# Holding the square of chunk 2's decays behind the last N eviction of chunk 1 in a chunked RWKV and mixture-of-experts kernel

## The chip, the cores and the metric

The kernel runs on one core of one Trainium2 chip. The metric is device microseconds of one execution, lower is better. The kernel before was run three times, and the numbers of the profile come from one further, profiled execution of the same program.

## The reference

The first half is a linear attention with a matrix state for each batch and head (4 batches, 8 heads, 768 steps, head size 40):

```python
for t in range(S):
    y[:, :, t] = np.einsum('bhd,bhde->bhe', rt, state)
    Sa = np.einsum('bhde,bhe->bhd', state, at)
    state = state * wt[:, :, None, :] - np.einsum('bhd,bhe->bhde', Sa, bt)
    state = state + np.einsum('bhd,bhe->bhde', vt, kt)
```

The second half sends each of the 3072 tokens (320 wide) to the one of 8 experts with the largest gate, computes relu(x @ w1[e]) @ w2[e] with 1024 hidden units, and scales the row by its gate weight and an output gate.

## The kernel before, in words

The 768 steps are cut into 12 chunks of 64 (`C`). Each chunk c goes through these stages:

- `scan(c)` (L103 to L124). The decays `w` and the tile `D` (a, k and b of the reference) are loaded by SyncE's queue (L109, L111). Two scans on VectorE (L116) give the running products `P` and `I`. ScalarE then squares the decays minus 0.9 **in place**, into the tile `w` itself, and keeps their sum (L119); that sum is only read at the very end, by a range check. `w`, `D`, `P` and `I` have one buffer each. So the next chunk's one-column memset of `w` on VectorE (L108) and its load of `w` (L109) have to wait until the square of this chunk is done.
- `prep(c)` (L137 to L249). The products scale a (`Av`, L184, L185, and 24 columns by ScalarE in L187) and k, b (`KBt`, L212). `Av` is spread into `Am`; for chunk 2 ScalarE (L201) and GpSimd (L203) do it, for later chunks transfers (L192). Three transfers a chunk, called the strips here, carry `Av` into the tile `LA` (L178). TensorE multiplies `KBt` by `Am` in six groups (L225); ScalarE copies each group out of PSUM in an "N eviction" of two parts (L236, the mark `s.mark['n', c]` ends as the very last of them) and an `LA` eviction (L238), and GpSimd masks the latter (L240). Transposes into `KB` and `WT` follow (L163, L165).
- `tinv(cs)` (L251). A triangular inverse on VectorE, by many small multiply and reduce pairs (L276, L278, L314 to L322), which starts with a transpose of `N` (L266 for chunks 0 and 1, which go alone; L271 for the later ones, which go in pairs).
- `crit(c, q)` (L367), two for each chunk. The recursion itself: alternating small matmuls (L379, L392), ScalarE moves out of PSUM (L383) and VectorE sums (L405), and the state for the next chunk (L430 to L439). `Dt` (L409) on GpSimd needs the strips of chunk c + 1.
- `tail` and the expert routing write the rows; the experts come last.

Below, square(c), N(c), w(c), D(c) and strips(c) are those of chunk c.

The order on each engine is fixed before the run. The function traces the work, `background()` feeding `prep`, `scan` and `tinv` between the steps of `crit`, and the framework's planner (`tile.TileContext(nc, schedule_with_timeline_sim=True)`, L1157) lays every engine's instructions, SyncE's transfers among them, into one queue each, by the times of its own model. The chip then takes each queue in that order. `tc.issue_after(x)` ties what is traced in its block, as far as it runs on the engine of x, behind x in that engine's queue. `scan(c + 1)` is traced right after `prep(c)` (L506 to L508), so when `scan(2)` is traced, the last N eviction of chunk 1 has been traced and marked. The kernel before already holds square(1) and the copy in L187 of chunk 1 behind the last eviction of N(0).

Of the kernel before, what the change touches and what calls it, by code (L numbers as in the profile page):

```python
# [49 lines left out]
def pat(x, off, dims):  # L50

    return bass.AP(x.tensor, x.offset + off, [x.ap[0]] + [list(d) for d in dims])


class Att:
# [47 lines left out]
    def scan(s, c):  # L103

        nc, V = s.nc, s.nc.vector
        n = 12 * 2 * 33
        w = s.p1.tile([120, n + 1], F32, name="w")
        V.memset(w[:, n:], 0.0)  # L108
        nc.sync.dma_start(out=w[:, 0:n], in_=s.win[c])  # L109
        s.D = s.p1.tile([120, 12, 3, C], F32, name="D")  # L110
        s.mark[c] = nc.sync.dma_start(out=s.D, in_=s.din[c]).ins  # L111
        P, I = (s.p1.tile([120, 12, 2, 33], F32, name=x) for x in "PI")
        Pf, If = (x.rearrange("p r h t -> p (r h t)") for x in (P, I))
        with s.tc.issue_after(s.mark['t', 0]) if c == 2 else ExitStack():
            for o, d in ((Pf, w[:, 0:n]), (If[:, ::-1], w[:, n:0:-1])):
                V.tensor_tensor_scan(out=o, data0=d, data1=s.rst, initial=0.0, op0=ALU.mult, op1=ALU.add)  # L116
        wq = pat(w, 1, [(33, 24), (1, 32)])
        with s.tc.issue_after(s.mark['n', 0]) if c == 1 else ExitStack():
            nc.scalar.activation(out=wq, in_=wq, func=AF.Square, bias=s.wb, accum_out=s.wsq[:, c:c + 1])  # L119
        rq = s.p1.tile([120, 24], F32, name="rq", bufs=2)  # L120
        V.reciprocal(out=rq, in_=P[:, :, :, 32])
        I3 = I.rearrange("p r h t -> p (r h) t")
        V.tensor_tensor(out=I3, in0=I3, in1=rq.unsqueeze(2).broadcast_to([120, 24, 33]), op=ALU.mult)
        s.Q = P, I, rq  # L124
# [12 lines left out]
    def prep(s, c):  # L137
# [45 lines left out]
        with s.tc.issue_after(s.mark['r', 0]) if c == 1 else ExitStack():  # L183
            (g if c > 1 else V).tensor_tensor(out=Av[:, :, 0:33], in0=a[:, :, 0:33], in1=I[:, :, 1, ::-1], op=ALU.mult)  # L184
            (g if c > 1 else V).tensor_tensor(out=Av[:, :, 33:64], in0=a[:, :, 33:64], in1=P[:, :, 0, 1:32], op=ALU.mult)  # L185
        with s.tc.issue_after(s.mark['n', 0]) if c == 1 else ExitStack():
            nc.scalar.copy(out=Av[:, :, 64:66], in_=P[:, :, :, 32])  # L187
        Ag = Av.rearrange("p (a g) t -> p a g t", a=2)
        if c and c != 2:
            for j in range(3):  # L190
                r, n = slice(40 * j, 40 * j + 40), 6 if j < 2 else 4
# [26 lines left out]
        for side in range(2):  # L218
            Am = s.Am[:, side]
            yield  # L220
            for g0 in range(0, 6, 2):
# [6 lines left out]
                for h in range(2):  # L228
                    r = slice(64 * side + 32 * h, 64 * side + 32 * h + 32)
                    n = C - 32 * h  # L230
# [356 lines left out]
class Moe:  # L587
# [346 lines left out]
    def experts(s, ctx, verdict):  # L934
# [21 lines left out]
        def unit(e, t0, nt, prep):  # L956

            for _ in s.expert(nt, W[e], T[e, t0], lambda: s.hp, ps1, ps2) if (e, t0) != (0, 0) else s.E0:
                next(prep, None)
            for _ in prep:  # L960
                pass
# [199 lines left out]
```

## Time and profile before

| what | us |
|---|---|
| median of 3 runs (lowest, highest) | 682.52 (681.66, 682.61) |
| the profiled execution | 678.98 |
| its span in the profile | 677.2 |
| TensorE matmul busy in the span | 630.9 (93%) |
| VectorE busy | 464.9 (69%) |
| ScalarE busy | 340.2 (50%) |
| GpSimd busy | 233.8 (35%) |

All times in the rows are microseconds from the start of the span, and durations are microseconds unless marked ns. PE is TensorE's matmuls, PEld its weight loads, DVE VectorE, ACT ScalarE, POOL GpSimd, SP SyncE (SPq its queue of transfers). A timeline row gives the start, the duration, the engine, the line of the kernel, the operation and its tiles; "x2" merges two neighbours, and the bracket at the end says how long the engine had been idle before and what ended the idleness.

### The profile page before, as it was taken

The numbers are of one execution on the slowest core, as the hardware profiler recorded it, in microseconds if no ns is written. First come the engines' busy times: TensorE is split into PE (matmuls) and PEld (weight loads), VectorE is DVE, ScalarE is ACT, GpSimd is POOL, SyncE is SP. The second block draws the span as 40 slices with busy tenths as digits, with TensorE's granted clock in tenths as the row PEclk, the third lists the DMA queues.
The fourth block names the chain that finished last, engine by engine and source line by source line (L and its number), as shares of the span: only waits on it lengthen the run. The fifth ranks groups of instructions, "written<-read, shape, count | busy, mean of one in ns | idle before, by whom it ended". The sixth has DMA issues, their size and how long they took to land. (4 is left out here: it accounts for less than half of the span.)

```text
span 677.2 us, 21154 instructions
## 1 busy us (share of the span) xinstructions
PE 630.9 (93%) x8871; PEld 564.3 (83%) x8871; DVE 464.9 (69%) x911; ACT 340.2 (50%) x783; POOL 233.8 (35%) x337
## 2 busy tenths in 40 slices
PE   7787988898999999989999889899999999999996
PEld 6475877787988888878889779799999999999985
DVE  8868689969986997699399654374774545654231
ACT  2577762784378357637743354253573435343120
POOL 9655321341144258314204111335342333211112
PEclk9667999999999999999999979999999999999999
DMA  5995763276346726643224752263774344431001
GB/s 141 179 184 132 175 156 82 78 165 168 98 128 166 157 80 168 173 97 99 83 80 126 194 165 76 58 195 85 213 203 152 115 135 134 150 103 34 19 11 32
DMA packets 56305, 84.45 MB, mean 125 GB/s; under 512 B 26848, under 2 KB 43515, under 8 KB 54763
## 3 DMA queue, kind: packets, MB, share of 16 engines
q1 hardware_dynamic: 52331, 74.05, 42.3%
q0 software_dynamic: 3872, 8.97, 4.7%
q8 instruction: 72, 1.18, 0.7%
q14 instruction: 30, 0.25, 0.1%
HBM read 67.59 MB, written 8.96 MB: 113 GB/s over the span
## 5 line engine op out<-in xcount | busy, mean ns | idle before, releaser
L863 DVE SCALAR_TENSOR_TENSOR hl<-ph,hh 128x480 fp32r<-128x480 f32 (+1 forms) x74 | 41.3, 567 | 65.4 <-ACT hh L862 65.3
L862 ACT ACTIVATE hh<-ph 128x480 fp32r<-128x480 f32 (+1 forms) x74 | 36.7, 501 | 93.5 <-PE ph L858 93.1
L878 POOL DMA_INDIRECT out_dram<-y,ti x32 | 34.3, 1073 | 141.5 <-DVE y L877 80.8
L873 PE MATMUL po<-w2h,hh 128*120 128x320 f32 x256 | 78.3, 311 | 0.2 <-ACT hh L862 0.2
L874 PE MATMUL po<-w2l,hh 128*120 128x320 f32 x256 | 77.6, 309 | 0.0
L858 PE MATMUL ph<-xh,w1h 128*128 128x480 f32 (+1 forms) x222 | 76.1, 347 | 0.3 <-DVE mem L704 0.3
L858 PE MATMUL ph<-xl,w1h 128*128 128x480 f32 (+1 forms) x222 | 75.7, 344 | 0.0
L875 PE MATMUL po<-w2h,hl 128*120 128x320 f32 x256 | 74.9, 308 | 0.0
L225 PE MATMUL pl<-Am,KBt 120*128 120x192 f32 (+1 forms) x288 | 62.9, 352 | 7.7 <-ACT LA L238 6.2
L240 POOL TENSOR_SCALAR_AFFINE_SELECT LA<-LA 64x192 f32<-64x192 f32 x144 | 55.2, 418 | 40.2 <-ACT LA L238 38.8
L383 ACT ACTIVATE As<-pa,hq 128x320 f32<-128x320 f32 x80 | 42.1, 528 | 47.2 <-PE pa L392 36.0
L236 ACT ACTIVATE N<-pl 32x192 f32<-32x192 f32 (+1 forms) x138 | 51.6, 374 | 26.3 <-PE pa L392 12.2
L225 PEld LDWEIGHTS pl<-Am,KBt 120*128 120x128 f32 x288 | 47.1, 205 | 13.4 <-ACT LA L238 8.7
L480 PE MATMUL pY<-KB,M 128*64 128x64 f32 (+1 forms) x768 | 53.3, 225 | 3.0 <-DVE M L468 3.0
L479 PE MATMUL pY<-Sd,R 128*64 128x64 f32 (+1 forms) x704 | 53.9, 227 | 0.0
L392 PE MATMUL pa<-As,Tc 64*32 64x40 f32 x1792 | 51.1, 204 | 2.9 <-ACT As L383 2.1
L730 POOL DMA_INDIRECT tab<-rec,si x24 | 29.9, 1245 | 67.6 <-DMA tab<-rec,si 45.5
L464 PE MATMUL pM<-R,VU 128*128 128x128 f32 x384 | 52.3, 287 | 0.9 <-ACT VU L456 0.8
L480 PEld LDWEIGHTS pY<-KB,M 128*64 128x64 f32 x768 | 46.9, 138 | 6.6 <-DVE M L468 3.4
L838 POOL DMA_INDIRECT xg<-xd,ti x32 | 35.8, 1118 | 44.6 <-PE px L821 32.7
L392 PEld LDWEIGHTS pa<-As,Tc 64*32 64x32 f32 x1792 | 40.3, 112 | 12.8 <-issue 3.8
L858 PE MATMUL ph<-xh,w1l 128*128 128x480 f32 (+1 forms) x148 | 50.7, 344 | 0.0
(198 smaller groups left out, 1571.2 us busy)
## 6 DMA issues: line engine op xcount, KB each, us to landing
D<-in_din_dram SPq DMA_DIRECT2D x12, 1080.0 KB
st<-in_w_dram SPq DMA_DIRECT2D x16, 512.0 KB
st<-in_w_dram SPq DMA_DIRECT2D x16, 480.0 KB
XS<-in_vt_dram SPq DMA_DIRECT2D x24, 256.0 KB
XU<-in_vt_dram SPq DMA_DIRECT2D x24, 256.0 KB
VU<-in_vl_dram SPq DMA_DIRECT2D x24, 208.0 KB
w<-in_win_dram SPq DMA_DIRECT2D x12, 371.2 KB
st<-in_w_dram SPq DMA_DIRECT2D x16, 256.0 KB
```

The lines of the kernel that those rows point to most:

```text
L225: nc.tensor.matmul(pl[:, i, 0:nj], KBt[:, 6 * side + g0 + i].rearrange("p n t -> p (n t)"), Am[:, g0 + i:g0 + i + 6 * nj - 5:6, 0:64], sta ...
L236: s.mark['n', c] = nc.scalar.activation(out=nn, in_=pn, func=AF.Copy, scale=-1.0).ins
L240: g.affine_select(out=la[:, :, i], in_=la[:, :, i], pattern=[[0, nj], [1, C]], base=0, channel_multiplier=-1, compare_op=ALU.is_gt, fill=0.0)
L383: s.mark['as'] = nc.scalar.activation(out=x, in_=pa, func=AF.Copy, scale=s.hq[:, h:h + 1]).ins
L392: nc.tensor.matmul(pa[o + w:o + w + 32, i], m(p)[o:o + 64], x[o:o + 64, i, :], start=start, stop=True, tile_position=(o, o + w), skip_grou ...
L464: nc.tensor.matmul(pM[:, i], VU[:, h0 + i].rearrange("p n t -> p (n t)"), R[:, :, h0 + i], start=True, stop=True)
L479: nc.tensor.matmul(o, R[:, side, i, :], Sf[:, 40 * i:40 * i + w], start=True, stop=False)
L480: s.mark['y'] = nc.tensor.matmul(o, Ms[i // 4][:, i % 4, side, :], Kf[:, k:k + w], start=not c, stop=True).ins
L858: nc.tensor.matmul(ph, l, r, start=(i == 0), stop=(i == 7))
L873: nc.tensor.matmul(po, hh[f][:, ts_], w2h[:, f], start=(f == 0), stop=False)
L874: nc.tensor.matmul(po, hh[f][:, ts_], w2l[:, f], start=False, stop=False)
L875: nc.tensor.matmul(po, hl[f][:, ts_], w2h[:, f], start=False, stop=(f == 7))
```

## The change

The block around the square now holds for chunks 1 and 2, each behind the last N eviction of the chunk before; the block around the copy in L187 is written another way and still holds for chunk 1 alone.

```diff
-        with s.tc.issue_after(s.mark['n', 0]) if c == 1 else ExitStack():
+        with s.tc.issue_after(s.mark['n', c - 1]) if c in (1, 2) else ExitStack():
             nc.scalar.activation(out=wq, in_=wq, func=AF.Square, bias=s.wb, accum_out=s.wsq[:, c:c + 1])
...
-        with s.tc.issue_after(s.mark['n', 0]) if c == 1 else ExitStack():
+        with s.tc.issue_after(s.mark['n', c - 1]) if c in (1,) else ExitStack():
             nc.scalar.copy(out=Av[:, :, 64:66], in_=P[:, :, :, 32])
```

## Rows read from the trace of the kernel before

**Rows 1.** Timeline of ScalarE, 44 to 49 us: start, duration, engine, line, operation.

```profile
44.21 0.94 ACT L119 ACTIVATE w<-w,wb 120x768 f32<-120x768 f32 x1
45.14 0.51 ACT L383 ACTIVATE As<-pa,hq 128x320 f32<-128x320 f32 x1
...
46.69 0.48 ACT L238 ACTIVATE LA<-pl 64x384 f32<-64x384 f32 x1
47.20 0.66 ACT L236 ACTIVATE N<-pl 32x256 f32<-32x256 f32 x2
47.88 0.38 ACT L238 ACTIVATE LA<-pl 64x256 f32<-64x256 f32 x1
48.37 0.94 ACT L201 ACTIVATE Am<-Av,hj 120x768 f32<-120x768 f32 x1
```

**Rows 2.** Timeline of TensorE's matmuls and weight loads, 43 to 47 us.

```profile
43.43 2.50 PE L225 MATMUL pl<-Am,KBt 120*128 120x192 f32 x8
...
45.86 0.82 PEld L392 LDWEIGHTS pa<-As,Nm 64*32 64x32 f32 x32 [0.23 <-ACT As L383]
```

**Rows 3.** Timeline of VectorE, 45 to 49 us.

```profile
45.30 0.06 DVE L108 MEMSET w<- 120x1 f32 x1 [3.57 <-ACT w L119]
46.92 0.97 DVE L405 TENSOR_TENSOR As<-As,pa 32x320 f32<-32x320 f32 x2 [1.56 <-PE pa L392]
47.92 1.11 DVE L266 STREAM_TRANSPOSE tmpf<-N 128x512 f32<-128x512 f32 x1
```

**Rows 4.** Timeline of SyncE's queue of transfers, 45 to 54 us.

```profile
45.26 0.34 SPq L109 DMA_DIRECT2D w<-in_win_dram  x1
48.36 2.56 SPq L178 DMA_DIRECT2D LA<-Av  x3
53.48 0.35 SPq L111 DMA_DIRECT2D D<-in_din_dram  x1
```

**Rows 5.** Timeline of GpSimd, 47 to 62 us.

```profile
47.37 0.97 POOL L184 TENSOR_TENSOR Av<-D,I 120x396 f32<-120x396 f32 x1
48.44 3.77 POOL L203 TENSOR_SCALAR Am<-Av,hj 120x768 f32<-120x768 f32 x2
52.28 1.89 POOL L240 TENSOR_SCALAR_AFFINE_SELECT LA<-LA 64x192 f32<-64x192 f32 x4
56.88 1.58 POOL L409 TENSOR_TENSOR Dt<-LA 40x32 f32<-40x32 f32 x1 [2.71 <-DMA LA<-Av]
...
61.42 0.92 POOL L185 TENSOR_TENSOR Av<-D,P 120x372 f32<-120x372 f32 x1 [2.22 <-DMA D<-in_din_dram]
```

**Rows 6.** Transfers by tile, over the whole span: count and KB of each.

```profile
D<-in_din_dram SPq DMA_DIRECT2D x12, 1080.0 KB
...
w<-in_win_dram SPq DMA_DIRECT2D x12, 371.2 KB
...
LA<-Av SPq DMA_DIRECT2D x24, 123.8 KB
...
LA<-Av SPq DMA_DIRECT2D x12, 82.5 KB
```

**Rows 7.** Stretches: start:end, length, busy time (instructions) by engine, clock, DMA share, GB/s.

```profile
54.70:61.20 6.50, 1.89 (x40) 1.35 (x38) 6.47 (x12) 4.00 (x12) 2.25 (x3) 0.90 0.82 190
...
87.20:134.00 46.80, 39.18 (x881) 33.86 (x882) 45.57 (x89) 24.74 (x62) 11.11 (x22) 1.00 0.42 107
```

**Rows 8.** Timelines of VectorE, ScalarE and TensorE, 54 to 62 us.

```profile
54.74 1.80 DVE L116 TENSOR_TENSOR_SCAN I<-w,rst 120x792 f32<-120x792 f32 x1
...
55.51 0.49 ACT L238 ACTIVATE LA<-pl 64x384 f32<-64x384 f32 x1
58.41 0.94 ACT L119 ACTIVATE w<-w,wb 120x768 f32<-120x768 f32 x1 [2.41 <-DVE P L116]
...
59.79 0.82 ACT L236 ACTIVATE N<-pl 32x384 f32<-32x384 f32 x2
...
61.16 1.65 PE L225 MATMUL pl<-Am,KBt 120*128 120x192 f32 x4 [4.40 <-ACT LA L238]
```

**Rows 9.** Timeline of VectorE, 87 us.

```profile
87.17 1.98 DVE L271 STREAM_TRANSPOSE Ns<-N 128x1024 f32<-128x1024 f32 x1 [5.45 <-ACT N L236]
```

## The prediction

> **What bounds the kernel now.** I read the timelines of the engines first, for the square is one instruction and only its neighbours can tell what it holds up. Square(2) stands on ScalarE at 44.21, takes 0.94, and the next instruction starts at 45.14: ScalarE goes from one to the next without a gap, so whatever is queued behind the square comes 0.93 late [rows 1]. Behind it stand a move of the recursion (L383), and the last N evictions of chunk 1, which end at 47.20 + 0.66 = 47.86 [rows 1]; the inverse of chunk 1 on VectorE starts at 47.92, on their heels [rows 3].
>
> Then I followed that stage to the one that sets the pace. The inverse of chunks 2 and 3 starts at 87.17, after VectorE has waited 5.45 for the last eviction of N(3) [rows 9], and from 87.2 to 134.0 VectorE is busy 45.57 of 46.80 us [rows 7]. So up to 87 the path to watch is the preparation of chunks 2 and 3, and a microsecond lost there is a microsecond lost later, since VectorE has only 1.2 us of idleness to make up from. In that path there is one large hole: TensorE waits 4.40 us, until 61.16, for an LA eviction of chunk 2. That eviction and the N eviction before it, at 59.79, stand on ScalarE behind square(3), for which ScalarE itself waited 2.41 us, until the scans of chunk 3 were done [rows 8]. The first of these scans starts at 54.74 and needs w(3). And w(3) is loaded into the tile that square(2) has to leave first. That is the thread from the change to the end.
>
> **The change, part by part.** The second edit does nothing: the copy is held for chunk 1 alone, as before. The first edit bites, for square(2) now stands at 44.21, ahead of the eviction at 47.20 [rows 1]. No operation is added or taken away; one ScalarE instruction with the reading of its sum moves by some 3 us, and with it the release of `w`.
>
> *What moves up.* The L383 move could start at 44.21, 0.93 earlier. It feeds the matmuls at 45.86, but these are on an engine that is busy with eight matmuls of chunk 1 until 43.43 + 2.50 = 45.93, and their weight loads had waited only 0.23 for the move [rows 2]. So the sum in L405 comes at most about 0.23 earlier, at 46.69 instead of 46.92. The last N eviction can end 0.93 earlier, at 46.93, but the transpose that waits for it stands behind L405 on VectorE, which by then ends at 46.69 + 0.97 = 47.66 [rows 3]. So the inverse starts some 0.2 to 0.3 earlier. Bounds for the gain: 0.93, if the planner puts the transpose ahead of L405, and 0, if the 0.23 is lost again in the busy VectorE behind. I take 0.2, from the row that binds (the weight load's wait).
>
> *Where the square goes.* With the evictions 0.93 earlier, ScalarE is through with the LA eviction at 48.26 - 0.93 = 47.33. The next in its queue, L201, cannot start before GpSimd's product ends at 47.37 + 0.97 = 48.34 [rows 1, 5]. That leaves 1.0 us, and the square takes 0.94. So I cost the square in its new place at nothing, with that wait as its cover. If the planner puts other ready copies there and the square later, up to 0.94 lies on ScalarE again, which is the loss there was before, at another place.
>
> *The memset of w on VectorE.* It waited 3.57 us for the square, at 45.30 [rows 3]. The square would now end at about 48.3. If the memset kept its place ahead of L405, that sum would slip from 46.92 to about 48.4, by 1.4 us, and the inverse behind it too. I take 0: the planner knows the later release and has the transposes and sums of that stretch to put ahead of it. The upper end stays 1.4.
>
> *The load of w(3).* It is issued at 45.26 now, and would be at about 48.3 [rows 4]. The delay of the issue as such costs little, since the transfer queues are backlogged: D(3), 1080 KB, is issued at 53.48 and GpSimd waits for it until 61.42, which is 7.9 us; at the 190 GB/s of that stretch its own bytes take 5.8 us, so some 2 us of other transfers were still ahead of it even then [rows 4 to 7]. What counts is the order on SyncE. The strips of chunk 2, 2 x 123.8 + 82.5 = 330 KB, are issued at 48.36, once GpSimd has made `Av` at 48.34 [rows 4 to 6]. On the chip's times w(3) and the strips would come ready within 0.1 us of each other. In the planner's they need not: it put GpSimd's product and both products of L203 ahead of the masks of L240 [rows 5], although the first LA eviction for these masks ended on the chip at 47.17, before that product began [rows 1]. So in its model `Av` seems to be ready early, and the strips are then likely to be issued first. If w(3) is ahead of the strips, it lands as before and costs 0. If it is behind, it is the last of that backlog, as the strips are now, which land at 56.88 by GpSimd's wait [rows 5]; the scan could then start 56.88 - 54.74 = 2.1 us later, less whatever w(3) had to spare before, which no row shows. By bytes alone it is 330 KB at 190 GB/s, 1.8 us. So the bounds are 0 and 2.1. I take 0.5 for the likeliest case: w(3) ahead of the strips, or behind them with most of the 1.8 us spare.
>
> [...]
>
> *The sum.* Minus 0.2 and plus 0.5 is plus 0.3. The durations are from the profiled execution, 678.98 us with a span of 677.2, which lies 3.5 us under the median of 682.52; I carry the difference over to the median: 682.8. This case by itself runs from 682.3 (0 for the load) to 683.9 (1.6 for it).
>
> **The rivals.**
>
> *Faster: the late w(3) makes the planner reorder ScalarE.* A scan that it sees later makes square(3) ready later, and then the N eviction of chunk 2 that stands at 59.79 may go ahead of it. Nothing else would hold it: ScalarE is free from 55.51 + 0.49 = 56.00 [rows 8]. The eviction comes up to 3.8 us earlier, and with it goes most of TensorE's wait of 4.40. For it speaks that the planner chose this order by its own times, which the chip contradicts by 2.41 us of idle ScalarE; a small shift can tip it. Against it, that its scan may have had time to spare. Time: 682.5 - 3.8 = 678.7, and half of it, 680.6, if only one of the two groups goes ahead.
>
> *Slower: w(3) is issued behind the strips and nothing else is reordered.* The place is the scan at 54.74; the price is 2.1 us on scan, square(3), evictions and TensorE's wait, each of which waits for the one before with no slack in the rows [rows 8], less the 0.2 won: 682.5 + 1.9 = 684.4. It decides as soon as w(3) lands after 54.74 by more than 1.6. For it speaks the argument on `Av` above; against it, that the planner may then fill VectorE otherwise.
>
> *It does nothing that reaches the end:* the evictions move, VectorE's order keeps its pace, w(3) lands in time: 682.5.
>
> **How the numbers follow.** About 0.2%, 1.4 us, is what a measurement of this kernel can tell from no change. The forecast gets 0.36: of that 0.27 stay within 0.2%, 0.05 are faster (the whole 0.93, and something on ScalarE behind it), 0.04 slower. The faster rival gets 0.31, the slower 0.30, no effect 0.03. That makes faster 0.05 + 0.31 = 0.36, same 0.27 + 0.03 = 0.30, slower 0.04 + 0.30 = 0.34. Both signs hold most of the chance, so the range has to reach both rivals: from 678.7, the full gain of the first, to 685.8, which is the slower rival and the 1.4 of the memset on top of it. What lies outside is a reordering of later chunks that no row before can price. The likeliest case's own range is 682.3 to 683.9.
>
> **What would show it.** Right: square(2) on ScalarE between the LA eviction and L201, near 47.3; the last N eviction of chunk 1 ending near 46.9; the transpose of L266 within 0.3 of 47.9 and still behind L405; the wait of TensorE near 61 still about 4.4, and L271 within 1 us of 87.2. Wrong towards faster: the N evictions of chunk 2 ahead of square(3), the wait near 61 under 2 us, L271 at 84 or before. Wrong towards slower: SyncE with the strips ahead of w(3), VectorE idle ahead of the first scan of chunk 3, which starts after 56, and L271 near 89; or the memset ahead of L405 with an idle VectorE until 48. If L271 moves and the end does not, the carrying from 87 to the end is what failed.

## The result, and the profile after

The changed kernel takes 686.49 us (median of 5 runs, 685.4 to 689.76) against 682.52 for the kernel before, ratio 1.007 [1.0049, 1.0092]. The profiled execution took 685.40 us with a span of 683.7; the one of before took 678.98 with 677.2, which is 3.5 under its own median, so the 6.4 us between the two profiles are not the size of the effect. Two repeats of the changed kernel, further down, give 1.0029 [0.9995, 1.0062] and 1.0038 [1.0014, 1.0061]. All ratios leave out the few executions that lie more than 1.5% above the fastest of their kernel. It is slower, by 2 to 4 us, and the forecast of 682.8 with a range to 685.8 was wrong.

**The stage around the change went much as foreseen.** Timeline of ScalarE in the kernel after, 44 to 49 us (start, duration, engine, line, operation):

```profile
44.45 0.53 ACT L383 ACTIVATE As<-pa,hq 128x320 f32<-128x320 f32 x1
...
46.52 0.66 ACT L236 ACTIVATE N<-pl 32x256 f32<-32x256 f32 x2
47.20 0.38 ACT L238 ACTIVATE LA<-pl 64x256 f32<-64x256 f32 x1
47.60 0.94 ACT L119 ACTIVATE w<-w,wb 120x768 f32<-120x768 f32 x1
...
48.93 0.93 ACT L201 ACTIVATE Am<-Av,hj 120x768 f32<-120x768 f32 x1
```

Against [rows 1], the last N evictions end 0.68 earlier, and the square stands between the LA eviction and L201. VectorE, and SyncE's queue, in the same stretch:

```profile
46.00 0.97 DVE L405 TENSOR_TENSOR As<-As,pa 32x320 f32<-32x320 f32 x2 [4.26 <-PE pa L392]
47.21 1.10 DVE L266 STREAM_TRANSPOSE tmpf<-N 128x512 f32<-128x512 f32 x1 [0.24 <-ACT N L236]
48.34 0.42 DVE L267 TENSOR_SCALAR tmpf<-tmpf,hm 128x256 f32<-128x256 f32 x1
48.71 0.06 DVE L108 MEMSET w<- 120x1 f32 x1
```

```profile
48.64 2.56 SPq L178 DMA_DIRECT2D LA<-Av  x3
51.31 0.44 SPq L109 DMA_DIRECT2D w<-in_win_dram  x1
54.13 0.32 SPq L111 DMA_DIRECT2D D<-in_din_dram  x1
```

The transpose L266 comes 0.71 earlier than in [rows 3], the memset waits for nothing, and w(3) is now issued behind the strips [rows 4]. Timelines of VectorE, ScalarE and TensorE, 55 to 62 us, and VectorE at 87:

```profile
55.48 1.81 DVE L116 TENSOR_TENSOR_SCAN I<-w,rst 120x792 f32<-120x792 f32 x1
...
59.19 0.94 ACT L119 ACTIVATE w<-w,wb 120x768 f32<-120x768 f32 x1 [2.18 <-DVE P L116]
...
60.36 0.82 ACT L236 ACTIVATE N<-pl 32x384 f32<-32x384 f32 x2
...
61.73 1.65 PE L225 MATMUL pl<-Am,KBt 120*128 120x192 f32 x4 [3.96 <-ACT LA L238]
...
87.70 1.98 DVE L271 STREAM_TRANSPOSE Ns<-N 128x1024 f32<-128x1024 f32 x1 [5.56 <-ACT N L236]
```

The scan starts 0.74 later than in [rows 8], and nothing shows it waiting for w(3). L271 starts 0.53 later than in [rows 9]; that is within the 0.9 us by which L266 alone wanders between executions of one kernel (47.92 and 48.87 in two of the kernel before). **So at 87 us hardly anything has been lost.**

**The loss stands behind it.** From the first L271 to the next one (chunks 4 and 5) the kernel before takes 62.41 us and the kernel after 63.91. Between the two, much on VectorE has changed its place, the scans of the next chunk and the state updates (L434, L435) among it. Three of the moves are taken up here and in the experiments, all among the operations of the inverse: the two M products of one half-chunk (L468) and one x product (L482). First VectorE in the kernel before, then in the kernel after:

```profile
115.88 0.69 DVE L314 TENSOR_TENSOR tmpf<-Ns,Ut 128x512 f32<-128x512 f32 x1
116.49 0.68 DVE L319 TENSOR_REDUCE Yt<-tmpf 128x32 f32<-128x512 f32 x1
117.20 0.69 DVE L468 TENSOR_TENSOR M<-pM,mM 128x512 f32<-128x512 f32 x1
117.81 0.68 DVE L319 TENSOR_REDUCE Yt<-tmpf 128x32 f32<-128x512 f32 x1
118.40 0.47 DVE L434 TENSOR_TENSOR tmS<-XS,pS 40x320 f32<-40x320 f32 x1
118.80 1.28 DVE L314 TENSOR_TENSOR tmpf<-Ns,Ut 128x512 f32<-128x512 f32 x2
120.00 0.68 DVE L468 TENSOR_TENSOR M<-pM,mM 128x512 f32<-128x512 f32 x1
```

```profile
118.62 0.69 DVE L319 TENSOR_REDUCE Yt<-tmpf 128x32 f32<-128x512 f32 x1
119.22 0.68 DVE L314 TENSOR_TENSOR tmpf<-Ns,Ut 128x512 f32<-128x512 f32 x1
119.94 0.48 DVE L434 TENSOR_TENSOR tmS<-XS,pS 40x320 f32<-40x320 f32 x1
120.34 0.68 DVE L314 TENSOR_TENSOR tmpf<-Ns,Ut 128x512 f32<-128x512 f32 x1
120.94 0.68 DVE L468 TENSOR_TENSOR M<-pM,mM 128x512 f32<-128x512 f32 x1
...
122.53 0.68 DVE L468 TENSOR_TENSOR M<-pM,mM 128x512 f32<-128x512 f32 x1
```

In the kernel after, the first M product stands behind one L319, two L314 and an L434 more than in the kernel before, counted from the same operation of the inverse. None of these brackets a wait: VectorE is simply busy, and the product's turn comes late. TensorE, which multiplies by M in L480, shows the price. Its timeline in the kernel before, then in the kernel after:

```profile
117.95 0.27 PE L480 MATMUL pY<-KB,M 128*64 128x64 f32 x1 [1.23 <-DVE M L468]
...
120.73 0.27 PE L480 MATMUL pY<-KB,M 128*64 128x64 f32 x1 [0.91 <-DVE M L468]
```

```profile
121.67 0.27 PE L480 MATMUL pY<-KB,M 128*64 128x64 f32 x1 [2.27 <-DVE M L468]
```

And the stretches around it in the kernel after (start:end, length, busy time by engine in the order PE, PEld, DVE, ACT, POOL, then granted clock, DMA share, GB/s):

```profile
120.00:122.00 2.00, 0.33 (x10) 0.33 (x12) 2.00 (x4) 0.03 (x1) 0.00 (x0) 1.00 0.41 94
122.00:124.00 2.00, 2.00 (x59) 1.88 (x56) 1.97 (x5) 0.00 (x0) 0.00 (x0) 0.59 0.00 0
124.00:126.00 2.00, 2.00 (x46) 1.91 (x44) 2.00 (x4) 1.58 (x4) 1.53 (x3) 0.56 0.04 8
```

TensorE is busy for 0.33 of two microseconds, and the granted clock then is 0.59 and 0.56 for the next four. In the kernel before it is 1.00 throughout [rows 7]. The same two views show the same wait of 2.27 in the repeats of the kernel after; the fall of the clock is there in one of the two (`again_after2`: 0.57 from 124 to 128; `again_after`: 1.00 from 120 to 130).

### The profile page after: what moved, and what is told of

Same layout as the page of the kernel before. It is cut to its first block, busy times and chain, and to the rows that moved or that the text cites. A ratio compares the mean times of both kernels' runs of the same rounds, so it can differ in the third digit from the quotient of the medians.

```text
span 683.7 us, 21155 instructions
## 1 busy us (share of the span) xinstructions
PE 631.8 (92%) x8871; PEld 565.1 (83%) x8871; DVE 465.2 (68%) x911; ACT 339.3 (50%) x783; POOL 232.8 (34%) x337
## 5 line engine op out<-in xcount | busy, mean ns | idle before, releaser
L225 PE MATMUL pl<-Am,KBt 120*128 120x192 f32 (+1 forms) x288 | 60.9, 344 | 7.5 <-ACT LA L238 6.1
L480 PE MATMUL pY<-KB,M 128*64 128x64 f32 (+1 forms) x768 | 54.8, 226 | 2.7 <-DVE M L468 2.3
L225 PEld LDWEIGHTS pl<-Am,KBt 120*128 120x128 f32 x288 | 45.6, 200 | 12.8 <-ACT LA L238 8.0
L464 PE MATMUL pM<-R,VU 128*128 128x128 f32 x384 | 52.2, 287 | 1.2 <-ACT VU L456 1.1
L480 PEld LDWEIGHTS pY<-KB,M 128*64 128x64 f32 x768 | 47.9, 139 | 6.4 <-issue 2.6
L392 PE MATMUL pa<-As,Tc 64*32 64x40 f32 x1792 | 50.4, 204 | 2.5 <-ACT As L383 1.4
L392 PEld LDWEIGHTS pa<-As,Tc 64*32 64x32 f32 x1792 | 39.8, 111 | 12.3 <-issue 3.4
```

Source lines behind the costliest of these rows:

```text
L225: nc.tensor.matmul(pl[:, i, 0:nj], KBt[:, 6 * side + g0 + i].rearrange("p n t -> p (n t)"), Am[:, g0 + i:g0 + i + 6 * nj - 5:6, 0:64], sta ...
L392: nc.tensor.matmul(pa[o + w:o + w + 32, i], m(p)[o:o + 64], x[o:o + 64, i, :], start=start, stop=True, tile_position=(o, o + w), skip_grou ...
L464: nc.tensor.matmul(pM[:, i], VU[:, h0 + i].rearrange("p n t -> p (n t)"), R[:, :, h0 + i], start=True, stop=True)
L480: s.mark['y'] = nc.tensor.matmul(o, Ms[i // 4][:, i % 4, side, :], Kf[:, k:k + w], start=not c, stop=True).ins
```

## The experiments

**How an order was tried.** The planner's queues can't be edited in the source, so each test kernel carries a written-out order of every engine's instructions, SyncE's transfers among them, and ties each to the one ahead of it before the planner runs. The work is the same in all. No kernel was run with the planner's own order written out and nothing moved. The common edit:

```diff
+def pin_order(tc):
...
+    raw = zlib.decompress(base64.b85decode(ORDER))
+    ins = {i.name: i for i in tc.nc.cur_bb.bb.instructions}
...
+        for a, b in zip(ids, ids[1:]):
+            tc.add_manual_dep(ins[f"I-{b}"], f"I-{a}", mybir.DependencyInfo(mybir.DependencyClass.NoSync, mybir.DependencyReason.DATA),
+                              reason="pin_order")
...
+        pin_order(tc)
```

Below, a diff under "queue" is one of the order that this pins. All differences between the queues of the two kernels lie between 44 and some 135 us; behind that they are identical. "Early" is what stands ahead of the first L271, "late" what stands behind it.

**1. The move alone.** First the kernel before and after again, unedited; then the kernel before with nothing but the square moved, and with the memset and the load of w(3) moved too, where the planner put them.

`again_before`: 

> The kernel before, unchanged, profiled a second time. It tells how much of the 6.5 us between the two spans is one execution's chance. Theory A (the planner's other order between 44 and 135 us loses 2.0 us, the rest is chance in the chain of scatters to `tab`): the fifth transpose of L336 starts at 376.1 within 0.3 again, while the wait of VectorE for the table (L888), at 390.87 in the first profile, comes 1 to 4 us later. Theory B (all 6.5 us belong to the change): both times within 0.5 us of the first profile, span 677 to 678.

`again_after`: 

> The changed kernel, unchanged, profiled a second time. Theory A: the fifth transpose of L336 at 378.1 within 0.3 again, the table's arrival (L888, 395.23 in the first profile) 1 to 3 us off either way. Theory B: both within 0.5 us of the first profile, span near 683.7.

```diff
 ScalarE's queue (only_square, square_memset_load)
-L119(2) L383 ... L236 L236 L238 ... L201
+L383 ... L236 L236 L238 L119(2) ... L201
 VectorE's queue (square_memset_load)
-L108 L405 L266 L267
+L405 L266 L267 L108
 SyncE's queue (square_memset_load)
-L109 L178 L178 L178 L111
+L178 L178 L178 L109 L111
```

`only_square`: 

> Every engine's queue is written out in the order of the kernel before; only square(2) is moved on ScalarE, to the place it has in the changed kernel, behind the LA eviction that follows the last N eviction of chunk 1. The memset of w stays ahead of L405 on VectorE, the load of w(3) ahead of the strips. Theory A (the other order is what costs, the move by itself little): the memset is reached at about 48.5, L405 and L266 behind it 1.4 to 1.6 late, and that is the price, L271 at 87.5 to 88.7, L336 of chunks 2 and 3 at 132.2 to 133.5, time 0.3 to 1.6 us over the kernel before. Theory C (the late load of w(3) is what costs): the load is ahead of the strips, so nothing is lost, within 0.3 us of the kernel before or faster.

`square_memset_load`: 

> As only_square, but the memset of w stands behind L267 and the load of w(3) behind the strips of chunk 2, as in the changed kernel; all else in the order of the kernel before. Theory A: L405 and L266 come 0.7 to 0.9 early, the load of w(3) costs at most 0.7 at the scan (55.5 in the changed kernel against 54.7), L271 within 0.6 of 87.2 and L336 of chunks 2 and 3 within 0.6 of 131.9; time within 0.6 us of the kernel before. Theory C: the late load of w(3) by itself loses what the changed kernel loses: L336 of chunks 2 and 3 near 134.3, time 2 us or more over the kernel before.

Measured: 0.9987 [0.9961, 1.0012] for the kernel before against itself, 1.0029 [0.9995, 1.0062] for the kernel after, 1.0003 [0.9972, 1.0034] for the square alone, 1.0006 [0.9974, 1.0037] with memset and load. VectorE with the square alone:

```profile
48.78 0.06 DVE L108 MEMSET w<- 120x1 f32 x1 [7.01 <-ACT w L119]
48.85 0.97 DVE L405 TENSOR_TENSOR As<-As,pa 32x320 f32<-32x320 f32 x2
49.85 1.10 DVE L266 STREAM_TRANSPOSE tmpf<-N 128x512 f32<-128x512 f32 x1
```

The memset, left where it was, holds the transpose to 49.85, 1.93 later than in [rows 3]. With memset and load moved too, VectorE shows where w(3) lands:

```profile
47.27 1.10 DVE L266 STREAM_TRANSPOSE tmpf<-N 128x512 f32<-128x512 f32 x1 [0.24 <-ACT N L236]
...
56.19 1.81 DVE L116 TENSOR_TENSOR_SCAN I<-w,rst 120x792 f32<-120x792 f32 x1 [1.21 <-DMA w<-in_win_dram]
```

The scan waits 1.21 for w(3) and starts 1.45 later than in [rows 8]. Of the 1.45, 0.30 is the later start of the whole stretch in that execution (ScalarE is free behind the LA eviction at 44.51, and in [rows 1] at 44.21). Yet neither kernel is slower at the end by more than the interval. **The move of the square, in whole or in part, is worth nothing that shows**, though the intervals, which reach 1.0034 and 1.0037, don't exclude a loss of 2 us by themselves.

The scan's wait for a w(3) put behind the strips can't be put down to the order alone, for the load is also issued 6 us later (51.40 against 45.26). The wait is 1.21 here, not the whole 2.1 of the prediction's bound.

**2. Halves.** The early order of the kernel after with the late order of before, and the reverse.

```diff
 every engine's queue (early_after)
-all of before
+up to L271 of chunks 2 and 3: as in after; behind it: as in before
 every engine's queue (late_after)
-all of before
+up to L271 of chunks 2 and 3: as in before; behind it: as in after
```

`early_after`: 

> The counterpart: the square is held and every queue has the order of the changed kernel up to L271 at 87 us, and the order of the kernel before from there. Theory A: L271 at 87.5 to 88.6, the stretch to the next L271 back at 61.7 to 62.4, and the time within 0.8 us of the kernel before. Theory D: the stretch stays at 63.6 or more.

`late_after`: 

> The square of chunk 2 is not held, and every queue keeps the order of the kernel before up to the transpose of L271 at 87 us (and what runs beside it on the other engines); from there each queue has the order of the changed kernel. Theory A (the loss sits in the other order after 87): from that transpose to the next one of L271, which is 62.4 and 61.9 us in the two profiles of the kernel before and 63.9 and 64.0 in the two of the changed kernel, this takes 63.6 to 64.2. Theory D (the order after 87 is harmless, and the loss is a delay handed on from before): 61.8 to 62.5.

Measured: 0.9990 [0.9959, 1.0021] and 1.0005 [0.9971, 1.0038]. Neither half alone shows a loss, and this settled nothing: both intervals still hold 1.002. The profile of `early_after` had one more thing, its granted clock by stretches:

```profile
62.00:70.00 8.00, 7.78 (x82) 5.96 (x81) 4.31 (x7) 6.07 (x16) 4.17 (x11) 0.50 0.19 62
70.00:77.00 7.00, 7.00 (x67) 6.21 (x67) 3.33 (x6) 3.00 (x8) 0.36 (x2) 0.50 0.14 46
```

Until 77 it runs at 0.50, where the kernel after has 1.00 from 70 on, and L271 comes at 91.53. Of the ten profiles with the early order of after two were like that (the other is `gp_after`, with 0.53 from 70 to 77 and L271 at 91.36); the other eight reach L271 at 87.94 on average, against 87.90 for eight profiles with the early order of before that have no such stretch. Two in ten against none is no proof that the order does it.

**3. Another cause, which fell.** Near 396 us the kernel after shows a wait of TensorE of 5.21 us for the sum L434 (2.50, near 392, in the kernel before). L434 stands on VectorE behind two copies of the routing table, which wait for a transfer (5.92 in the kernel after, 3.13 in the kernel before). The copies were moved to GpSimd in both kernels (`q` is GpSimd where the experts start early, and nothing at the other place):

```diff
-        nc.vector.tensor_copy(out=tb, in_=tr.rearrange("p t f -> p f t"))
+        (q or nc.vector).tensor_copy(out=tb, in_=tr.rearrange("p t f -> p f t"))
...
-        nc.vector.tensor_copy(out=ti, in_=tb[:, 0:2])
+        (q or nc.vector).tensor_copy(out=ti, in_=tb[:, 0:2])
```

`gp_before`: 

> The kernel before, with the two small copies of the table of the first experts (L888, L890) on GpSimd instead of VectorE; the program is the same in every other place. On VectorE they wait for the transfer of the table (390.87 in the first profile) with the state updates of L434 behind them, and TensorE waits 2.50 us for those. Theory E (the scatters and the table's transfer, whose length changes from one execution to the next, come into the time through this wait): TensorE's wait at L430 near 391 is gone, the time falls by 1.5 to 5 us, and the runs lie closer together. Rival F: GpSimd or the gather behind it takes the place of the wait, or the end is set elsewhere: within 1 us of the kernel before, same spread.

`gp_after`: 

> The same two copies moved in the changed kernel. Theory A with E: the difference to gp_before is the loss up to 150 us alone, 1.7 to 2.7 us. Theory B (the change costs 4 us or more, part of it in the wait for the table): 3.5 us or more over gp_before, or, if that wait was the part, 2 us where the plain kernels differ by 4.

Measured: 0.9993 [0.9968, 1.0019] and 1.0031 [1.0005, 1.0057]. The wait for L434 is gone from `gp_before`, the time is not, and the distance between the two kernels is unchanged: 683.22 - 680.11 = 3.1 us. That wait is not the cause.

**4. The three products, swapped.** The kernel after with only these three put back, and the kernel before with only these three moved. M1 and M2 are the L468 of the half-chunk above.

```diff
 VectorE's queue (after_m)
-L319 L405 L405 L319 L314 L434 L314 M1 L319 L435 M2 L322
+L319 M1 L405 L405 L319 L314 L434 L314 M2 L319 L435 L322
 VectorE's queue (before_m)
-L314 L319 M1 L319 L434 L314 L314 M2 L435 L319 L322
+L314 L319 L319 L434 L314 L314 M1 L435 L319 M2 L322
 VectorE's queue, the x product (before_m; after_m has the reverse)
-L276 L482 L278 L314 L314 L319
+L276 L278 L314 L314 L482 L319
```

`again_after2`: 

> The kernel after the change, unedited, to fix the size of the loss. Theory (the move itself is neutral; the planner's re-ordering of queues up to 135 us costs time, more in some executions than in others): 1.5 to 4 us above the kernel before, ratio 1.002 to 1.006. Rival (the late load of w(3) alone costs it, 0.2 to 2.1 us in the prediction): no more than 2 us. In the profile TensorE waits about 2.3 us at one product of L468 near 122.

`after_m`: 

> The order of the kernel after on every engine, but three products on VectorE (the two M products of L468 and the x product of L482) go back to the places they have in the kernel before relative to the inverse of chunks 2 and 3. Theory (these late products starve TensorE between 100 and 130): its single waits there fall from 2.27 and 1.30 to about 1.2 and 0.9, the granted clock stays at 1.00 from 100 to 130, L271 to L336 takes 44.3 to 45.0 us instead of 46.6, and the time is 1 to 2 us under that of the kernel after. Rival (the early order up to 87 us costs it): no change against the kernel after, 1.5 to 4 us above the kernel before.

`before_m`: 

> The order of the kernel before on every engine, but the same three products on VectorE stand as late as in the kernel after. Theory (late products): a wait of TensorE of about 2.3 us near 118 to 122, the granted clock under 1.00 somewhere between 100 and 130 in some executions, L271 to L336 45 to 46.6 us instead of 44.3 to 44.8, and the time 0.3 to 1.9 us above the kernel before. Rival (the early order): the time of the kernel before within 0.3 us.

`early_after2`: 

> A repeat, with more runs, of the kernel whose queues are those of the kernel after up to L271 of chunks 2 and 3 and those of the kernel before behind it. Rival (the early order costs it): 1.5 to 4 us above the kernel before. Theory (late products): within 1 us of the kernel before by the median; where the granted clock stays at 0.50 beyond 70 us, as in the first execution of it, L271 comes near 91, else near 88.

Measured, all against the same runs of the kernel before: 1.0038 [1.0014, 1.0061] for the kernel after, **0.9999 [0.9965, 1.0032] with the three products put back**, **1.0040 [1.0014, 1.0065] for the kernel before with these three late**, 0.9997 [0.9970, 1.0023] for the early order alone. The swap goes both ways: the first step brings back the time of the kernel before with all the rest as in the kernel after, and the second makes a loss as large as that of the change with all the rest as in the kernel before. The first half is the weaker: the intervals of `again_after2` and `after_m` overlap, and their medians lie 2.4 us apart. Timelines of VectorE and TensorE in `before_m`, then its stretches:

```profile
120.05 0.67 DVE L468 TENSOR_TENSOR M<-pM,mM 128x512 f32<-128x512 f32 x1
...
120.77 0.27 PE L480 MATMUL pY<-KB,M 128*64 128x64 f32 x1 [3.40 <-DVE M L468]
```

```profile
118.00:120.00 2.00, 0.00 (x0) 0.00 (x0) 1.97 (x4) 0.00 (x0) 0.00 (x0) 1.00 0.47 107
120.00:122.00 2.00, 1.23 (x31) 1.23 (x32) 2.00 (x5) 0.00 (x0) 0.00 (x0) 0.83 0.00 0
122.00:124.00 2.00, 2.00 (x43) 1.79 (x42) 1.97 (x4) 0.00 (x0) 0.00 (x0) 0.50 0.03 8
124.00:126.00 2.00, 2.00 (x53) 1.90 (x52) 1.01 (x3) 0.51 (x2) 0.49 (x1) 0.82 0.02 7
```

Two microseconds without one matmul, then a clock of 0.83, 0.50 and 0.82, and then VectorE idle for half of 124 to 126: it waits in turn for TensorE. The wait is 3.40 and not the expected 2.3: M1 comes 2.85 later than in the kernel before (120.05 against 117.20). So `before_m` overdoes what the planner did, and its loss, 2.4 us by the medians, is above the expected 0.3 to 1.9.

**5. Which product, and whether they could stand better.** In `after_2m` only M1 and M2 go back, in `after_x` only the x product; `late_after2` repeats a half; `before_e` puts M1 and M2 earlier than the kernel before has them.

```diff
 VectorE's queue (before_e)
-L405 L405 L314 L319 M1 L319 L434 L314 L314 M2 L435
+L405 L405 M1 L314 L319 L319 L434 M2 L314 L314 L435
```

`after_2m`: 

> The kernel after, with only the two M products of L468 put back to the places of the kernel before on VectorE; the x product of L482 stays late. If the M products carry the loss: no wait of 2.27 us before TensorE's L480 near 122, the wait of about 1.3 us before L650 near 106 stays, time at the kernel before within 0.2%. If the x product carries it: 1.5 to 3 us above the kernel before, granted clock under 1.00 between 104 and 120 in some executions.

`after_x`: 

> The kernel after, with only the x product of L482 put back; the two M products stay late. If the M products carry the loss: the wait of about 2.27 us before L480 stays, L271 to L336 takes 45 to 47 us, granted clock often under 1.00 between 120 and 130, time 1.5 to 3 us above the kernel before. If the x product carries it: the kernel before within 0.2%.

`late_after2`: 

> A repeat of the queues of the kernel before up to L271 of chunks 2 and 3 with those of the kernel after behind it. Its three products are late, so by the theory of late products it takes 2 to 3 us more than the kernel before, as the kernel with these three alone moved did; the first measurement of it, plus 0.3 with an interval of plus or minus 2.3, would have been low by chance. If it again lies within 0.2% of the kernel before, the late products cost only together with something else.

`before_e`: 

> The kernel before, with the two M products of L468 two inverse operations earlier on VectorE than it has them: ahead of the L314 at 115.88 and of the L314 at 118.80. TensorE's waits of 1.23 and 0.91 before L480 fall to under 0.4. The inverse on VectorE does the same work in another order, and the granted clock is 1.00 there already, so the theory expects the time of the kernel before within 0.2%; if single waits of 1 us on TensorE cost time by themselves, 1 to 2 us less.

Measured: 1.0001 [0.9980, 1.0022] with M1 and M2 back, 1.0018 [0.9989, 1.0047] with x back, 1.0006 [0.9982, 1.0030] for the late half, and **0.9968 [0.9944, 0.9991]** for the earlier products, 678.80 against 681.35 us. With the two M products back the time is that of the kernel before. That x counts for nothing is likely but not shown: the medians of `after_2m` and `after_x` lie 1.6 us apart, and the interval of either holds the other's ratio. The late half again lies low, as it should not if the products alone made 2 to 3 us whatever stands ahead of them; by its expectation this speaks for a cost that comes only together with something else. `before_e` missed its expectation to the better side. Of TensorE's two waits in it the first is gone, and the second remains:

```profile
116.61 0.27 PE L480 MATMUL pY<-KB,M 128*64 128x64 f32 x1
...
119.36 0.27 PE L480 MATMUL pY<-KB,M 128*64 128x64 f32 x1 [0.87 <-DVE M L468]
```

The last two runs ask whether the gain of `before_e` holds, alone and in the kernel after:

```diff
 VectorE's queue (after_e; x as in before)
-L405 L405 L319 L314 L434 L314 M1 L319 L435 M2 L322
+L405 L405 M1 L319 L314 L434 M2 L314 L319 L435 L322
```

`before_e2`: 

> A repeat of the kernel before with its two M products of L468 two inverse operations earlier. If single waits of TensorE of about 1 us in this stretch cost time by themselves: again some 2 us (0.1 to 0.5%) under the kernel before, L271 to L336 under 44 us. If the first result was chance: the kernel before within 0.2%.

`after_e`: 

> The kernel after, with the x product of L482 where the kernel before has it and the two M products still earlier, right behind the L405 and the L434 that precede them. If early M products gain about 2 us whatever the early order: 0.1 to 0.5% under the kernel before, 4 us under the kernel after. If the gain belongs to the order of the kernel before: within 0.2% of the kernel before. TensorE's wait before L480 near 121 falls from 2.27 to under 0.9.

Measured: 0.9963 [0.9938, 0.9989], 679.73 against 682.35, and 0.9999 [0.9976, 1.0022]. The gain holds in the queues of the kernel before and is not there in those of the kernel after, where M1 at 119.26 had to wait 0.91 for its own matmuls. **`before_e` beats the kernel before**, twice; the kernel after was not run beside it.

**What all profiles say together.** The stretch from the first L271 to the second starts behind the early order and ends far ahead of the routing's transfers. Its rows, in the columns of the stretches above, for the kernel before, the kernel after, `before_m`, `after_m` and `before_e`:

```profile
87.17:149.58 62.41, 54.76 (x1150) 47.30 (x1151) 55.29 (x103) 37.42 (x95) 16.38 (x36) 1.00 0.50 119
```

```profile
87.70:151.61 63.91, 55.84 (x1157) 48.31 (x1151) 55.51 (x102) 37.17 (x95) 16.09 (x33) 0.97 0.49 115
```

```profile
87.66:152.88 65.22, 56.06 (x1150) 48.54 (x1150) 54.36 (x102) 37.35 (x95) 16.99 (x36) 0.97 0.48 114
```

```profile
87.87:149.00 61.13, 54.04 (x1156) 46.83 (x1150) 54.83 (x102) 37.17 (x95) 17.82 (x37) 1.00 0.52 123
```

```profile
87.88:148.23 60.35, 54.55 (x1150) 47.22 (x1150) 54.44 (x102) 37.41 (x95) 17.47 (x36) 1.00 0.52 123
```

The length less TensorE's busy time is its idle time: 7.65, 8.07, 9.16, 7.09 and 5.80. Of the 1.5 us that the kernel after loses, 1.1 are longer matmul time, at a mean clock of 0.97, and 0.4 are waiting; in `before_m` 1.3 and 1.5. A clock under 1.00 is not needed for the loss: `again_after` takes 63.95 at a clock of 1.00, with 9.36 idle. `before_e` gains 1.85 by waiting less, at nearly the same busy time. By kind of kernel:

| place of the three products | profiles | L271 to L271, mean (lowest, highest) | clock under 1.00 between 100 and 130 |
|---|---|---|---|
| as in before (`after_2m`: M1 and M2 only) | 9 | 62.4 (61.1, 63.9) | 0 |
| late, all three | 7 | 64.4 (62.9, 65.4) | 5 |
| M1, M2 earlier (`before_e`, twice) | 2 | 60.5 (60.4, 60.6) | 0 |
| `after_e` | 1 | 62.4 | 1 |

`after_x`, with M1 and M2 late only, is not in the table. The 2.0 us between the first two lines is near what the times say of the change (2.0 and 2.6 us by the repeats of experiments 1 and 4, 4.8 by the first result). The lines overlap: `early_after` and `early_after2`, with the late order of before, take 63.47 and 63.87, so the products are not all that lengthens the stretch.

How much of it is left at the end varies: apart from the first result, seven comparisons with late products give ratios of 1.0005 to 1.0040, mean 1.0024, that is 1.6 us; the eight with products as in the kernel before (`after_2m` among them) give 0.9987 to 1.0006, mean 0.9997. One rival stays. Among the seven, the kernels with a written-out order that leaves M1 and M2 where the planner put them (`late_after`, `late_after2`, `after_x`) give 1.0005 to 1.0018, and those without one (`again_after`, `gp_after`, `again_after2`) 1.0029 to 1.0038; that writing the order out changes something by itself is thus not excluded by the times. The stretch speaks against it: of the kernels with a written-out order, three with late products take 64.4 and six with products as in before 62.4.

## Why the prediction was wrong

**Right, step by step.** The square found its gap on ScalarE and cost nothing there: L201 starts 0.31 after GpSimd's product is done (47.64 + 0.98 = 48.62), hardly a loss. The planner did put the strips ahead of w(3), as the argument on `Av` had it. The memset went behind the transposes. TensorE's wait near 61 is 3.96, "still about 4.4", and L271 is within 1 us of 87.2. Both rivals are out: no N eviction of chunk 2 passed square(3), and the slower rival's order came but cost at most 0.74 at the scan in place of 2.1. That the total was above its 684.4 in the first measurement is not its merit.

**Mis-sized.** The gain at L266 was taken at 0.2 and was about 0.95, the whole of the bound of 0.93. ScalarE is free for the square, or for what stands behind it, at 44.21 in the kernel before and at 44.45 in the kernel after, and L266 follows 3.71 and 2.76 later; the 0.71 between the two starts of L266 is this gain less the 0.24 by which the stretch runs later in that execution. The 0.2 came from the eight matmuls that hold L392 back until 45.93 [rows 2]. They ran at a granted clock of 0.50 there and took 2.50; in the kernel after it is 1.00 from 42 on, the eight take 0.92 + 0.71, and L392's weight loads start at 45.11. Over the other profiles the distance is 3.7 in every one with the early order of before. With the early order of after it is 2.8 in `again_after` too (45.07 to 47.88), at a clock of 0.50 from 40 to 45 and 0.98 from 45 to 50. Left in its place, the memset costs 1.6 at L266 by the same count (44.52 to 49.85 in `only_square`), a little above its upper end of 1.4. And w(3) was issued at 51.31 and not at 48.3, because it stands behind the 2.56 that SyncE takes to issue the strips [rows 4]. No run shows the 1.6 that the likeliest case's own range, up to 683.9, has for the load: the scan waited 1.21 for w(3) in `square_memset_load`, and no wait for it shows in the kernel after.

**The step that failed** is what the sum makes of the time behind 87. It carries what arrives at 87 unchanged to the end, since "VectorE has only 1.2 us of idleness to make up from", and so takes the kernel from there on to be VectorE's. The planner's other order behind 87 it puts at nothing: "a reordering of later chunks that no row before can price" stands outside the range. The runs showed in its place a loss that arises behind 87, with L271 hardly moved. The planner re-laid the queues as far as 135 us; in the kernel after, TensorE waits 2.27 for M1 and not 1.23, and the stretch is 2.0 us longer with late products (64.4 against 62.4). The three products moved late in the kernel before give 1.0040; put back in the kernel after they give 0.9999, M1 and M2 alone 1.0001.

Rows of the kernel before could have warned. TensorE waited 1.23 and 0.91 for two M products in the very stretch [rows 7] in which VectorE was taken for the limit, and what is put ahead of such a product lengthens the wait: in `before_m` M1 comes 2.85 later and the wait grows by 2.17. Both engines limit that stretch in turn: TensorE waits for M, and VectorE then waits for what TensorE makes of it (in `before_m` 0.99, until 125.22, for the product by M). `before_e` shows it most plainly, for it gains 2 us with the same work on VectorE.

In the profile of `before_m` the matmuls that make the M products' input (L464) end at 116.42 (115.26 + 1.16). VectorE takes M1 at 120.05, at its turn behind two L319, an L434 and two L314, while TensorE stands idle for 3.40 us.

**What stays open.** Why the planner moved just these products was not tried; its own times are in no trace. That late M products cost time, and early ones in the order of before save it, is shown; that they are the whole of the change's loss is not, for the other moves behind 87 were never tried by themselves. The late half without the early one shows less of a loss at the end than the same products elsewhere (1.0005 and 1.0006), though its two profiles took 65.12 and 62.88 us from L271 to L271; the intervals allow 1.003, and a cost that needs the early order as well is open. Whether the early order makes the long stretch at a clock of 0.50 to 0.53 ahead of 77 more frequent (two profiles in ten against none) is not settled either.

## What to carry to other kernels

When a tie is added and a planner lays the queues anew, compare the whole order of before and after first, engine by engine: the cost may stand 70 us behind the edit, in instructions that have nothing to do with it. An engine that is busy for 97% of a stretch need not be the only one that limits it: look at what the other engine waits for there, and whether the wanted instruction was ready and only stood behind others. Where another engine waits for a small product, try it further ahead in a long chain: here, two places earlier were worth 2 us in the queues of the kernel before, and nothing that shows in those of the kernel after.

## What the runs showed that was not expected

A lower clock does not follow on the same wait every time. Five of the seven profiles with late products show it fall after a wait of 1.3 to 3.4 us, to a mean of 0.83 to 0.87 over ten microseconds, two don't, at the same wait of 2.27; and in `after_e` it fell to 0.66 between 110 and 120 behind waits of at most 0.99. In `again_after2`, whose stretch is the longest of the seven (65.37), it fell already after a wait of 1.31 that ended at 105.99, for the x product. The stretches there and VectorE's timeline read:

```profile
104.00:108.00 4.00, 2.69 (x65) 2.27 (x59) 3.93 (x12) 1.45 (x3) 1.85 (x1) 0.89 0.54 132
108.00:112.00 4.00, 3.31 (x72) 2.87 (x70) 1.75 (x7) 1.23 (x3) 0.00 (x0) 0.69 0.02 4
```

```profile
111.39 0.99 DVE L405 TENSOR_TENSOR As<-As,pa 32x320 f32<-32x320 f32 x2 [2.23 <-PE pa L392]
```

VectorE idles 2.23 for the recursion at a clock of 0.69, and 0.74 at the same place in the kernel after, where the clock is 1.00 from 104 to 112: here the lower clock on one engine goes with more waiting on the other.

Part of the spread between executions of one program goes with the clock. Over 304 executions of the experiments up to `before_e`, each taken against the mean of its own kernel and chip, the longer ones have the lower mean granted clock (correlation -0.63, 3.5 us for 0.01 of clock). Kernels with the products as in before had 0.9707 on average (216 executions), those with late products 0.9673 (76): by that slope 1.2 us, out of the 1.6 that the ratios give. That is a correlation and not an experiment, but it holds in executions that no profile was read of.
